# Second layer three pairs of blocks behind the first in place of two, and a shorter hold in the planner

## The chip, the cores and the metric

The kernel runs on one core of one Trainium2 chip. The metric is the device time of one execution in microseconds (us). One execution was also recorded by the hardware profiler; the instruction times below are from that record.

## The reference

A gated scan over the sequence feeds two feed-forward layers, on 12160 tokens (2 sequences of 6080) of 256 channels. All data is float32.

```python
f = lower_bound + (1 - lower_bound) * sigmoid(f_logit)
for t in range(S):                       # per sequence and channel
    h = f[:, t] * h + (1 - f[:, t]) * x[:, t];  y[:, t] = h
x = y.reshape(12160, 256)
x = square(relu(x @ w_in1)) @ w_out1     # layer 1: 256 -> 2048 -> 256
h = x @ w_in2                            # layer 2: 256 -> 2048 -> 256
out = where(h > 0, h, exp(min(h, 0)) - 1) @ w_out2
```

## The kernel before

**Blocks and slots.** The tokens are cut into 24 blocks, the first of 384 tokens and the others of 512 (`block_sizes`, L39). Each layer of a block is worked in 8 slots, one for each 256 of the 2048 hidden channels. Every value that goes into a matmul is kept as two fp32r parts, a high and a low one, and a product is three matmuls (high x high, high x low, low x high).

**What a slot does.** TensorE (PE) makes the first product into a PSUM tile `pc`, and later the second product from the tile `g` into `acc`. For layer 1 of the first four blocks (`PLAIN`, L22) the first product is the ordinary one: 12 matmuls of 512 columns (L640). All other slots use a scheme with 7 products of sums in place of 8: `first` is 9 matmuls, `later` is 12 (both L626), and between the two ScalarE copies part of `pc` away (`snap`, L654). ScalarE (ACT) and VectorE (DVE) then build the hidden values: DVE adds L657, L662, L669, L665 and ACT copies L672; layer 1 takes relu and square on ACT (L675, L678, or L647 and L678 in plain slots); layer 2 takes ACT L682 and L685 (exp) and DVE L688 (elu). At last ACT rounds to the high part of `g` (L693), DVE subtracts for the low part (L698), and PE makes the second product (L725), `LAG` = 3 slots later or earlier if the slot has aged. There is one L698 for each slot, so the L698 of DVE number the slots: 1 to 16 are the first pair of blocks in layer 1, 17 to 32 the second pair, and so on.

**Around the slots.** Each block needs a scan (two halves: loads `fs` and `xs`, ACT tanh L553, DVE transposes L558, gate L564, feed L572, scan L585, carry L591) into the tile `F`, and its operand parts `xA` or `xB` (sums L492, L496, L500 for the seven-product scheme, the high part by ACT L508 or by DVE L510, the low part by DVE L516). Layer 1's result is spilled to DRAM (`xd`) and loaded again as layer 2's `F`. The weights are prepared once, on the way: ACT L383 and L386, DVE L389, L392, then a high part (DVE L411 or ACT L409) and a low part (DVE L415). The sums of weights for the seven-product scheme (DVE L337 to L340, L351 or ACT L349, L354) are kept in DRAM (`wd`) and streamed from there; layer 1's sums are made from a copy in DRAM (`rd`, loaded at L457).

**What sets the order.** Blocks are worked in pairs, one layer of a pair being a run of 16 slots. The list of runs (L254 to L258) begins with `BEHIND` pairs of layer 1, then alternates a pair of layer 2 with the next pair of layer 1, and ends with `BEHIND` pairs of layer 2. PE's order follows from it alone (L267 to L292), and so do the due times of all steps: those of the weights are spread between the second pair's start and the first use (L836 to L844), and the scans of blocks from number `2 * BEHIND` on are held back to a slot of the run before (L870 to L875).

On the other engines the order is that of a planner (class `Order`, L47). It keeps for each engine the steps whose inputs it reckons ready. When the engine comes free, it looks at the steps that are ready then or within `HOLD` microseconds of the earliest, and takes the one with the earliest due time:

```python
t0 = max(free[e], min(r.values()))
n = min((n for n, t in r.items() if t <= t0 + self.HOLD), key=lambda n: steps[n][2])
```

Steps that may run on either of two engines (L508 or L510, L411 or L409, L349 or L351) go to the one that takes them first. The order so found is written out as each engine's instruction stream, and each engine works through its own in that order.

Of the kernel before, what the change touches and what calls it, by code (L numbers as in the profile page):

```python
# [19 lines left out]
LAST = ()  # L20
LEAD = 2
PLAIN = 4  # L22
BEHIND = 2
LAG = 3
AGE = 10.0
ROW = 1 / 2185
# [20 lines left out]
class Order:  # L47
# [6 lines left out]

    SAME, CROSS, LOAD = 0.13, 0.22, 2.4
    RATE, AHEAD = 240.0, 2.0
    HOLD = 0.2
    SLACK = 0.3

    def __init__(self):  # L60
# [33 lines left out]
    def run(self):  # L94
# [33 lines left out]
        while any(ready.values()):  # L128
            best = None
            for e, r in ready.items():  # L130
                if not r:
                    continue
                t0 = max(free[e], min(r.values()))
                n = min((n for n, t in r.items() if t <= t0 + self.HOLD), key=lambda n: steps[n][2])
                t0 = max(t0, r[n])
# [26 lines left out]
def kernel(  # L162
# [83 lines left out]
    def woven(m, bs, lead):  # L246
        a = [(m, bs[0], g) for g in range(KG)]
        b = [(m, x, g) for x in bs[1:] for g in range(KG)]
        got = a[:lead]
        for i in range(lead, KG + lead):  # L250
            got += a[i : i + 1] + b[i - lead : i - lead + 1]
        return got

    twos = [tuple(range(b, min(b + 2, NBK))) for b in range(0, NBK, 2)]  # L254
    runs = [(0, bs) for bs in twos[:BEHIND]]
    for i in range(BEHIND, len(twos)):
        runs += [(1, twos[i - BEHIND]), (0, twos[i])]
    runs += [(1, bs) for bs in twos[-BEHIND:]]  # L258
    slots = [s for m, bs in runs for s in woven(m, bs, LEAD)]
# [607 lines left out]
    for kind, s in pe_order:  # L867
        m, b, g = s
        if kind == "first":
            if m == 0 and g == 0:  # L870
                for h in range(2):

                    k = slots.index((0, b - b % 2, 0)) - SPREAD[b % 2 * 2 + h]
                    add_scan(n_scan, b, h, in_due[s] - 6.0, n_first[slots[k]] if b >= 2 * BEHIND else None)
                    n_scan += 1  # L875
# [45 lines left out]
```

## Time and profile before

| | |
|---|---|
| median of 3 runs | 2083.7 us (2083.47 to 2085.03) |
| the profiled execution's own time | 2083.75 us |
| its span, first to last instruction | 2082.0 us |
| PE busy | 2034.5 us, 98% of the span |
| DVE busy, ACT busy | 1732.3 us (83%), 1697.1 us (82%) |
| PE clock granted, mean | 0.996 of full |

PE is idle for 47.5 us of the span (2082.0 less 2034.5): at the start, in the stretch from 190 to 345 us, and in the last 20 us. In the 40 equal slices of the page, PE's first slice reads 3 and the rest 8 or 9.

### The profile page before, as it was taken

How to read it: one execution, taken by the hardware profiler on the slowest of the kernel's cores; microseconds unless marked ns; L12 is line 12 of the kernel's file. 1: busy time of each engine (PE TensorE's matmuls, PEld its weight loads, DVE VectorE, ACT ScalarE, POOL GpSimd, SP SyncE). 2: the span in 40 equal slices, each digit the busy share in tenths (PEclk: the TensorE clock that was granted, in tenths of full speed). 3: DMA queues.
4: the chain of work that ended last, by engine and by line, in shares of the span. 5: the costliest groups of instructions: out<-in, count | busy, mean ns of one | idle time of the engine just before them, and what ended most of it. 6: DMA issues, size and time to landing. Idle time of an engine off the chain costs nothing.

```text
span 2082.0 us, 36897 instructions
## 1 busy us (share of the span) xinstructions
PE 2034.5 (98%) x14640; PEld 1925.6 (92%) x14640; DVE 1732.3 (83%) x2830; ACT 1697.1 (82%) x2149; POOL 0.2 (0%) x4
## 2 busy tenths in 40 slices
PE   3999999999999999999999999999999999999998
PEld 3888889999999999999999999999999999999998
DVE  7977996996897798699699689779869968967876
ACT  5887778888888888889788888888888878888886
POOL 0000000000000000000000000000000000000000
PEclk8999999999999999999999999999999999999999
DMA  8787452442343344334244234334433424423321
GB/s 220 229 258 237 143 173 89 128 131 93 124 141 102 119 116 134 116 108 144 89 124 136 92 124 140 105 119 115 135 117 106 140 90 122 133 92 130 104 95 39
DMA packets 207540, 268.10 MB, mean 129 GB/s; under 512 B 110984, under 2 KB 135944, under 8 KB 207368
## 3 DMA queue, kind: packets, MB, share of 16 engines
q1 hardware_dynamic: 206784, 265.21, 40.7%
q8 instruction: 116, 1.90, 0.4%
q10 hardware_dynamic: 584, 0.53, 0.1%
q14 instruction: 56, 0.46, 0.1%
HBM read 221.91 MB, written 43.78 MB: 128 GB/s over the span
## 4 chain that ended last, share of the span: by engine, by line
PE 93%; DVE 4%; ACT 1%; DMA 1%; issue 0%; SPq 0%; DVEq 0%; ACTq 0%
PE acc L725 49%; PE pc L626 40%; PE pc L640 4%; DVE g L698 1%; DVE r L688 1%; DVE r L669 0%; DMA fs<-in_f_logit_dram 0%; DVE F L585 0%; ACT g L693 0%; DMA a<-rd 0%; DVE s L662 0%; ACT s L654 0%; SPq L328 0%; ACT e L682 0%; DVE r L665 0%
## 5 line engine op out<-in xcount | busy, mean ns | idle before, releaser
L725 PE MATMUL acc<-wo,g 128*128 128x256 f32 x4560 | 579.0, 282 | 4.4 <-DVE g L698 2.6
L725 PEld LDWEIGHTS acc<-wo,g 128*128 128x128 f32 x4560 | 560.1, 188 | 5.9 <-DVE g L698 3.9
L725 PE MATMUL acc<-g,wo 128*128 128x512 f32 (+1 forms) x2304 | 552.6, 389 | 0.0
L725 PEld LDWEIGHTS acc<-g,wo 128*128 128x128 f32 x2304 | 420.9, 188 | 78.5 <-DVE g L698 0.3
L626 PE MATMUL pc<-xB,ws 128*128 128x256 f32 x3696 | 486.9, 280 | 4.4 <-ACT s L654 3.6
L626 PE MATMUL pc<-xA,ws 128*128 128x256 f32 (+1 forms) x3696 | 485.8, 280 | 3.2 <-ACT s L654 2.0
L698 DVE TENSOR_TENSOR g<-r,g 128x1024 fp32r<-128x1024 f32 (+1 forms) x384 | 463.8, 1208 | 27.0 <-ACT g L693 24.7
L626 PEld LDWEIGHTS pc<-xB,ws 128*128 128x128 f32 x3696 | 463.6, 188 | 11.6 <-ACT s L654 4.2
L626 PEld LDWEIGHTS pc<-xA,ws 128*128 128x128 f32 x3696 | 463.0, 188 | 10.2 <-ACT s L654 2.4
L693 ACT ACTIVATE g<-r 128x1024 fp32r<-128x1024 f32 (+1 forms) x384 | 402.1, 1047 | 15.6 <-DVE r L688 8.6
L654 ACT ACTIVATE s<-pc 128x768 f32<-128x768 f32 (+1 forms) x352 | 283.5, 805 | 114.3 <-PE pc L626 112.8
L662 DVE TENSOR_TENSOR s<-pc,s 128x256 f32<-128x256 f32 (+1 forms) x352 | 147.8, 420 | 240.0 <-PE pc L626 238.7
L688 DVE SCALAR_TENSOR_TENSOR r<-e,r 128x1024 f32<-128x1024 f32 (+1 forms) x192 | 231.7, 1207 | 24.4 <-ACT e L685 23.7
L669 DVE TENSOR_TENSOR r<-pc,s 128x512 f32<-128x512 f32 (+1 forms) x352 | 241.8, 687 | 9.3
L682 ACT ACTIVATE e<-r 128x1024 f32<-128x1024 f32 (+1 forms) x192 | 202.0, 1052 | 15.0 <-DVE r L665 6.5
L685 ACT ACTIVATE e<-e 128x1024 f32<-128x1024 f32 (+1 forms) x192 | 202.1, 1052 | 6.0
L678 ACT ACTIVATE r<-r 128x1024 f32<-128x1024 f32 (+1 forms) x192 | 202.2, 1053 | 5.6
L675 ACT ACTIVATE r<-r 128x768 f32<-128x768 f32 x160 | 135.5, 847 | 77.7 <-DVE r L665 76.8
L672 ACT ACTIVATE r<-pc 128x256 f32<-128x256 f32 (+1 forms) x352 | 133.4, 379 | 79.5 <-DVE r L669 66.6
L657 DVE TENSOR_TENSOR s<-s 128x256 f32<-128x256 f32 (+1 forms) x352 | 147.1, 418 | 9.8 <-ACT s L654 0.8
L665 DVE TENSOR_TENSOR r<-s 128x256 f32<-128x256 f32 (+1 forms) x352 | 146.7, 417 | 0.0
L585 DVE TENSOR_TENSOR_SCAN F<-fT,carry,xT 128x256 f32<-128x256 f32 (+2 forms) x94 | 65.7, 728 | 0.3
(49 smaller groups left out, 832.1 us busy)
## 6 DMA issues: line engine op xcount, KB each, us to landing
ws<-wd SPq DMA_DIRECT2D x176, 896.0 KB, 5.0
out_dram<-o SPq DMA_DIRECT2D x47, 256.0 KB, 3.8
fs<-in_f_logit_dram SPq DMA_DIRECT2D x184, 64.0 KB, 3.9
xs<-in_x_dram SPq DMA_DIRECT2D x184, 64.0 KB, 2.1
xd<-o SPq DMA_DIRECT2D x46, 256.0 KB, 2.2
F<-xd SPq DMA_DIRECT2D x46, 256.0 KB, 3.3
st<-in_moe_w_out_dram SPq DMA_DIRECT2D x16, 512.0 KB, 4.6
wd<-wp SPq DMA_DIRECT2D x24, 256.0 KB, 4.0
```

The costliest lines, as they stand in the source:

```text
L626: nc.tensor.matmul(t["pc"][:, c], lhsT=ws[:, p, w], rhs=x_t[m, b][:, r, v], start=(which is FIRST_PRODUCTS and q == 0 and c in (1, 2)), st ...
L654: nc.scalar.activation(t["s"], t["pc"][:, 1:4], AF.Copy)
L657: nc.vector.tensor_tensor(t["s"][:, 1], t["s"][:, 1], t["s"][:, 2], op=ALU.add)
L662: nc.vector.tensor_tensor(t["s"][:, 0], t["pc"][:, 0], t["s"][:, 0], op=ALU.add)
L669: nc.vector.tensor_tensor(t["c"][:, 1:3], t["pc"][:, 2:4], u, op=ALU.add)
L678: nc.scalar.activation(t["r"], t["r"], AF.Square)
L682: nc.scalar.activation(t["e"], t["r"], AF.Relu, scale=-1.0)
L685: nc.scalar.activation(t["e"], t["e"], AF.Exp, scale=-1.0)
L688: nc.vector.scalar_tensor_tensor(t["r"], t["e"], 1.0, t["r"], op0=ALU.subtract, op1=ALU.max)
L693: nc.scalar.activation(t["g"][:, 0], t["r"], AF.Copy)
L698: nc.vector.tensor_tensor(t["g"][:, 1], t["r"], t["g"][:, 0].bitcast(F32), op=ALU.subtract)
L725: nc.tensor.matmul(a, lhsT=u, rhs=v, start=clear and k == 0, stop=two and k == 2, skip_group_check=True)
```

## The change

Two constants change. `BEHIND` goes from 2 to 3, `HOLD` from 0.2 to 0.1:

```diff
-BEHIND = 2
+BEHIND = 3
...
-    HOLD = 0.2
+    HOLD = 0.1
```

With `BEHIND` = 3 the runs are: layer 1 of pairs 0, 1, 2, then layer 2 of pair 0, layer 1 of pair 3, and so on, with three pairs of layer 2 at the end. The number of matmuls is the same. Both constants also move instructions on ACT, DVE and the DMA queue. DVE's high parts of x (L510) go from 27 to 34, ACT's (L508) from 65 to 58.

PE at the end of the second plain pair (`pc` first products, `acc` second products; `-` is the kernel before, `+` the changed one):

```order
 L725 MATMUL acc<-g,wo_70 128x512 x12
-L626 MATMUL pc<-xA,ws 128x192 x30
+L626 MATMUL pc<-xA,ws 128x256 x30
+L725 MATMUL acc<-g,wo_70 128x512 x12
+L626 MATMUL pc<-xA,ws 128x256 x21
+L725 MATMUL acc<-g,wo_70 128x512 x12
```

Where layer 2 of the first pair (192 columns wide) began, layer 1 of the third pair begins now.

DVE just before the first `xA` is ready, in the kernel before (`ws_235` and `ws_254` are the first layer's weights of slots 0 and 1, `F_221` the scan of block 0):

```order
L415 TENSOR_TENSOR ws_235<-a_198,ws_235 128x512
L392 SCALAR_TENSOR_TENSOR a_226<-st_193,a_226 128x512
L558 STREAM_TRANSPOSE fT_247<-fs_216 128x6x2x32
L564 TENSOR_SCALAR fT_247<-fT_247,ga_66,gb_67 128x192
L558 STREAM_TRANSPOSE xT_257<-xs_228 128x6x2x32
L564 TENSOR_SCALAR fT_247<-fT_247,ga_66,gb_67 128x192
L572 SCALAR_TENSOR_TENSOR xT_257<-fT_247,xT_257 128x2x192
L585 SCALAR_TENSOR_TENSOR F_221<-fT_247,carry_68,xT_257 128x192 x2
L591 COPY carry_68<-F_221 128x2
L389 SCALAR_TENSOR_TENSOR a_239<-a_239,st_204 128x512
L415 TENSOR_TENSOR ws_254<-a_226,ws_254 128x512
L516 TENSOR_TENSOR xA_269<-F_221,xA_269 128x4x192
```

The same place in the changed kernel (`ws_246` and `ws_269` are the weights of slots 1 and 2, `F_233` the scan):

```order
L411 CAST ws_246<-a_226 128x512
L415 TENSOR_TENSOR ws_246<-a_226,ws_246 128x512
L558 STREAM_TRANSPOSE fT_255<-fs_215 128x6x2x32
L558 STREAM_TRANSPOSE xT_257<-xs_228 128x6x2x32
L564 TENSOR_SCALAR fT_255<-fT_255,ga_66,gb_67 128x192
L389 SCALAR_TENSOR_TENSOR a_240<-a_240,st_204 128x512
L564 TENSOR_SCALAR fT_255<-fT_255,ga_66,gb_67 128x192
L392 SCALAR_TENSOR_TENSOR a_240<-st_204,a_240 128x512
L572 SCALAR_TENSOR_TENSOR xT_257<-fT_255,xT_257 128x2x192
L585 SCALAR_TENSOR_TENSOR F_233<-fT_255,carry_68,xT_257 128x192
L415 TENSOR_TENSOR ws_269<-a_240,ws_269 128x512
L585 SCALAR_TENSOR_TENSOR F_233<-fT_255,carry_68,xT_257 128x192
```

Ahead of the last scan instruction DVE now has eleven weight instructions (L389, L392, L411, L415) in place of six, and they stand between the scan's own steps; `L591` and `L516` come next.

DVE in a run of layer 2 in the middle of the kernel, where the next `xA` parts are made, before (`pc_12305` and `pc_12380` are first products of two slots that follow each other, `e` the exp):

```order
L698 TENSOR_TENSOR g_12356<-r_12250,g_12356 128x1024
L516 TENSOR_TENSOR xA_12320<-F_11674,xA_12320 128x1024
L662 TENSOR_TENSOR s_12347<-pc_12305,s_12347 128x256
L669 TENSOR_TENSOR r_12392<-pc_12305,s_12347 128x512
L688 SCALAR_TENSOR_TENSOR r_12349<-e_12376,r_12349 128x1024
```

And in the changed kernel:

```order
L662 TENSOR_TENSOR s_13164<-pc_13125,s_13164 128x256
L510 CAST xA_13215<-F_12507 128x1024
L688 SCALAR_TENSOR_TENSOR r_13166<-e_13194,r_13166 128x1024
L669 TENSOR_TENSOR r_13213<-pc_13125,s_13164 128x512
L657 TENSOR_TENSOR s_13243<-s_13243 128x256
L665 TENSOR_TENSOR r_13213<-s_13164 128x256
L516 TENSOR_TENSOR xA_13215<-F_12507,xA_13215 128x1024
```

The cast L510 was ACT's there, and now it and an elu stand between the two instructions that read one `pc`.

## Rows read from the trace of the kernel before

**Rows 1.** The page, part 1: busy us, share of the span, instructions.
```profile
PE 2034.5 (98%) x14640; PEld 1925.6 (92%) x14640; DVE 1732.3 (83%) x2830; ACT 1697.1 (82%) x2149; POOL 0.2 (0%) x4
```

**Rows 2.** Waits of PE, whole span: engine line <- releaser: us, times, longest.
```profile
PE pc L640 <- ACT xA L508: 20.5, 1, 20.5
PE pc L640 <- ACT xB L508: 10.1, 1, 10.1
```

**Rows 3.** Waits of PE from 190 to 345 us.
```profile
PE pc L626 <- ACT s L654: 5.6, 5, 1.7
PE pc L626 <- issue: 1.2, 1, 1.2
PE acc L725 <- DVE g L698: 1.0, 2, 0.8
PE pc L626 <- DVE r L669: 0.7, 1, 0.7
```

**Rows 4.** Windows of one run each: length, busy us by engine, clock, DMA share, GB/s.
```profile
209.00:293.67 84.67, 78.58 (x646) 76.78 (x644) 82.19 (x148) 64.36 (x90) 0.00 (x0) 1.00 0.50 158
...
378.34:463.01 84.67, 84.67 (x700) 84.14 (x699) 82.19 (x132) 71.33 (x90) 0.00 (x0) 1.00 0.44 131
463.01:547.68 84.67, 84.67 (x552) 77.31 (x551) 60.03 (x100) 70.06 (x91) 0.00 (x0) 1.00 0.32 106
```

**Rows 5.** DVE's groups by shape, 0 to 380 us: busy us, mean ns.
```profile
L392 DVE SCALAR_TENSOR_TENSOR a<-st,a 128x512 int32<-128x512 int32 x32 | 22.1, 690 | 0.8
L698 DVE TENSOR_TENSOR g<-r,g 128x768 fp32r<-128x768 f32 x16 | 15.2, 947 | 0.0
L411 DVE CAST wo<-a 128x512 fp32r<-128x512 f32 x15 | 6.4, 424 | 0.4
L337 DVE TENSOR_TENSOR a<-a 128x128 f32<-128x128 f32 x16 | 4.6, 287 | 8.0 <-DMA a<-rd 7.9
L510 DVE CAST xB<-F 128x1024 fp32r<-128x1024 f32 x2 | 1.4, 690 | 3.2 <-PE pc L640 3.2
```

**Rows 6.** Timeline of the start, ACT, DVE, PE: start us, us, instruction [idle before].
```profile
19.56 0.84 ACT L508 ACTIVATE xA<-F 128x768 fp32r<-128x768 f32 x1 [2.78 <-DVE F L585]
...
20.84 0.95 DVE L516 TENSOR_TENSOR xA<-F,xA 128x768 fp32r<-128x768 f32 x1
...
24.82 0.71 DVE L558 STREAM_TRANSPOSE xT<-xs 128x512 f32<-128x512 f32 x1
...
29.17 0.68 DVE L389 SCALAR_TENSOR_TENSOR a<-a,st 128x512 int32<-128x512 int32 x1
...
40.02 1.22 DVE L516 TENSOR_TENSOR xB<-F,xB 128x1024 fp32r<-128x1024 f32 x1
...
21.84 8.06 PE L640 MATMUL pc<-xA,ws 128*128 128x384 f32 x35 [0.70 <-DVE xA L516]
...
41.29 5.00 PE L640 MATMUL pc<-xB,ws 128*128 128x512 f32 x11 [0.51 <-DVE xB L516]
```

**Rows 7.** Timeline near the 14th slot, DVE's L698 and PE's second product.
```profile
101.71 1.22 DVE L698 TENSOR_TENSOR g<-r,g 128x1024 fp32r<-128x1024 f32 x1
...
106.83 2.90 PE L725 MATMUL acc<-g,wo 128*128 128x512 f32 x12
```

**Rows 8.** Waits of DVE, whole span.
```profile
DVE a L337 <- DMA a<-rd: 7.9, 3, 3.6
```

**Rows 9.** Timeline of PE at the first slot with seven products.
```profile
200.08 2.59 PE L626 MATMUL pc<-xA,ws 128*128 128x192 f32 x21 [0.74 <-ACT s L654]
```

**Rows 10.** Timeline late in a run of layer 2: PE's later product, DVE's L662.
```profile
797.62 2.66 PE L626 MATMUL pc<-xA,ws 128*128 128x256 f32 x21
...
801.05 0.42 DVE L662 TENSOR_TENSOR s<-pc,s 128x256 f32<-128x256 f32 x1
```

**Rows 11.** Waits of PE from 1990 us to the end.
```profile
PE acc L725 <- ACT g L693: 1.7, 1, 1.7
PE acc L725 <- DVE g L698: 1.6, 3, 0.8
```

## The prediction

> **What bounds the kernel now.** I read the busy shares first, then the windows of single runs, then the waits of PE, and last the timeline where PE waits. PE is busy for 2034.5 us of the 2082.0 us span [rows 1]. In the middle of the kernel one run of layer 2 and one of layer 1 take 84.67 us each, and PE is busy for all 84.67 us of both [rows 4]. There a change that keeps the number of matmuls can win nothing; it can only break something. What can be won is PE's 47.5 us of idle time. It lies in three places: 20.5 us before the first product and 10.1 us before the first product on `xB` [rows 2]; 5.6 + 1.2 + 1.0 + 0.7 = 8.5 us between 190 and 345 us [rows 3]; and 1.7 + 1.6 = 3.3 us at the end [rows 11]. The rest, some 5 us, is short waits at the start and the time after the last matmul.
>
> The 8.5 us have a cause that the windows show. A run of layer 2 alone keeps DVE busy for 82.19 of its 84.67 us; the first such run, from 209 us on, shows the same 82.19 us of DVE, but only 78.58 us of PE [rows 4]. In the order, between the 32nd and the 48th L698, DVE has weight work on top: 13 instructions of 512 columns (L389, L392, L415, L354), 3 casts and 16 sums of 128 columns. At 0.690, 0.424 and 0.287 us [rows 5] that is 9.0 + 1.3 + 4.6 = 14.9 us in a run that has some 2.5 us free. The narrower first block gives part of it back; the rest PE waits for, and clears it in the next run.
>
> **The third pair in between: -8.5 us.** The order of the changed kernel puts a run of layer 1 there. Such a run needs 60.03 us of DVE [rows 4]; the third sixteen slots now hold 14 of the long weight instructions, 3 casts and 8 sums, 9.7 + 1.3 + 2.3 = 13.3 us, so 73 of 84.67 us. The run of layer 2 after it holds no weight instruction at all and is like those of the middle, where PE doesn't wait. I take away all 8.5 us. The bounds are 0 and 8.5.
>
> **What is late in its place: +2.3 us.** Two places, from the order.
> - The first slot with seven products has its `first` and `later` products next to each other on PE, so PE must wait for the copy between them: 0.74 us today [rows 9]. The same gap stays. ACT now has an L508 for `xB` between the last plain slot's relu and that copy, an instruction of 0.84 us on the smaller block [rows 6]; I add 0.6 us of it and take 1.3 us.
> - The first layer's sums are due sooner and the scans of the third pair come a run earlier. Before its 14th L698 DVE has more to do than today: one scan of half a block, 29.17 - 24.82 = 4.35 us [rows 6]; four sums, 1.15 us; two casts L351, 0.85 us; three long instructions, 2.07 us; less two casts L411, 0.85 us [rows 5]. That is 7.6 us. Today this L698 ends at 102.93 and PE needs its tile at 106.83, 3.9 us later [rows 7]; with PE 3.1 us later (below) the cover is 7.0 us. So 0.6 us are left over. The sums read DRAM, and such reads made DVE wait up to 3.6 us [rows 8]; behind the waiting sum stands this very L698, and PE behind that. I take 0.8 us, bounds 0 and 4.2.
> - 0.2 us for others. Together 2.3 us; the bounds are 0.7 us, today's one wait, and 8.5 us, as much as goes.
>
> **The start: +3.1 us.** This is the shorter hold. DVE no longer keeps itself free for the next step of the scan, but fills each gap with a weight instruction of half a microsecond or more. Ahead of the end of block 0's scan stand eleven weight instructions in place of six: four more of 0.690 and one of 0.424 us [rows 5], 3.2 us. Two that stood between scan and L516 are among them, so L516 now waits only for ACT's L508, 0.84 us [rows 6]. I went through both queues instruction by instruction, with each duration as the timeline has it and with the gaps it shows between instructions that depend on each other and those that don't (the mixed order saves some of these gaps). L516 for `xA`, at 20.84 us today, comes 2.0 us later, and PE's 21.84 us with it [rows 6]. From there to L516 for `xB`, at 40.02 us today, two more L698 of 0.947 us stand in the way, one L389 more and one L411 less, 2.2 us [rows 5], of which the saved gaps give back more than half: 0.9 us more. PE starts on `xB` at about 44.2 us in place of 41.29 us [rows 6], 2.9 us later; with 0.2 us for ACT, which is late too, I take 3.1 us. By durations alone it would be 2.8 + 2.2 = 5.0 us; the least is the 2.0 us of the first part. A gain is excluded, since nothing is taken out of the way. From there to the 13th slot I found no product that comes late: DVE has the L698 of three slots behind it when PE resumes, and one today.
>
> After its wait PE runs at the lower of its two clocks: 5.00 us for 11 matmuls, 0.455 us each [rows 6], against 2.90 / 12 = 0.242 us later [rows 7]. That costs 2.3 us, and it will again, since the wait stays about as long: 0, bounds -1.2 and +1.2 us.
>
> **The middle: 0.** The hold changes the order of ACT and DVE in every run. DVE takes seven more casts L510 (27 to 34). In runs of layer 2 an L510 or a piece of a scan, and an elu, stand more often between L662 and L669, which together free a `pc`. Today, late in such a run, `later` ends at about 799.06 us and L662 starts at 801.05 us, 2.0 us behind [rows 10], and PE doesn't notice. PE needs that tile again one slot later, 84.67 / 16 = 5.3 us; L662 and L669 take some 1.1 us, so DVE may be about 4.2 us late. Adding up DVE's work slot by slot through one run of the new order, I find it at most 1.9 us behind, plus 1.8 us for a cast and an elu in front of L669: 3.7 us. It fits, barely.
>
> A rule of the Trainium skill speaks against the change here: its page Perfetto Trace Analysis, section Optimizing Scalar/DVE Operations, says that where DVE is saturated, moving work to Scalar may pay, and this change moves seven casts the other way. By that rule each would cost PE its 0.690 us, 4.8 us in all, and the sum would be 2085.1 us. By the rows PE is full beside a DVE at 82.19 of 84.67 us, so they cost nothing, and I go by the rows.
>
> **The end: -0.3 us.** The last run is as before; going through its last three slots I find the last product 0.3 us sooner. Bounds -1.6 and +1.0.
>
> **The sum.** The profiled execution took 2083.75 us, 0.05 us above the median of the runs, so nothing is corrected. 2083.75 - 8.5 + 2.3 + 3.1 - 0.3 = 2080.35, so 2080.3 us.
>
> **Rivals.**
> - *A cheap start.* The start costs 2.0 us and only the 0.7 us wait is new: 2083.75 - 8.5 + 0.7 + 2.0 - 0.3 = 2077.7 us. For it: DVE's two loads fall to 73 us of 84.67. Against it: the 14th slot has no cover to spare. 24%.
> - *The jam moves and doesn't go.* The second plain run takes over four half scans, 4 x 4.35 = 17.4 us, beside sums that wait for DRAM; DVE carries its lateness into the third run, whose first slots are its fullest, and PE waits 6 us there instead: 2084.0 us. Against it: that third run has 11 us to spare. 18%.
> - *The middle breaks: slower.* In the nine runs of layer 2 that also carry scans, L669 comes more than 4.2 us after `later` ends, once a run, and PE waits for its `pc`, say 1.2 us, the length of a single wait in [rows 3]: 9 x 1.2 = 10.8, so 2091 us. For it: 3.7 of 4.2 us; it decides from 0.5 us more. Against it: nothing in today's middle comes near. 12%.
>
> The forecast has 46%, with its own range from 2078.5 to 2082.3 us. A measurement of this kernel can tell about 0.2%, 4.2 us, from no change: below 2079.5 us is faster, above 2087.9 us slower. Faster: nearly all of the cheap start and a third of the forecast, 0.38. Slower: the broken middle, 0.11. Within: 0.51. The range from 2076.8 to 2085.2 us leaves out the broken middle and a few per cent of the bounds.
>
> **What would show it.** Right: PE's first wait near 23 us and its start on `xB` near 44 us; almost no PE wait from 210 us on; one wait for L654 near 203 us; runs of 84.67 us with PE full. Wrong: PE waits for L669 or L654 in runs of layer 2 after 400 us (broken middle), several waits between 200 and 300 us (the jam moved), or a start on `xB` near 41 or beyond 46 us.

## The result and the profile after

The changed kernel takes 2095.33 us in the median of four runs (2093.97 to 2096.27), the kernel before 2084.27 us in the four beside them: a ratio of 1.0053 with an interval of 1.0035 to 1.0070. It is slower, and 10 us above the upper end of the range. The profiled execution took 2094.52 us, its span is 2092.7 us, 10.7 us longer than before. The matmuls did not grow (PE is busy for 2036.0 us, 2034.5 before), so the loss is idle time. The waits of PE over the whole span answer to [rows 2, 3, 11]:

```profile
PE pc L640 <- ACT xA L508: 23.2, 1, 23.2
PE pc L640 <- ACT xB L508: 11.2, 1, 11.2
PE pc L626 <- ACT s L654: 9.0, 5, 4.4
PE acc L725 <- DVE g L698: 6.7, 11, 1.1
PE pc L640 <- ACT r L647: 1.6, 1, 1.6
```

Two lines carry the result. L654, the copy between `first` and `later`, is waited for 9.0 us in place of 5.6, once for 4.4 us. L698, the product that the output matmuls need, is waited for eleven times in place of five.

Where the 10.7 us are is read from the first L725 of each run of slots, in the two timelines:

| stretch | before, us | after, us | difference |
|---|---|---|---|
| up to the first L725 | 46.13 | 48.40 | +2.27 |
| plain runs and the first run with seven products in layer 1 (83.43 us elsewhere) | 164.25 + 83.43 | 254.75 | +7.07 |
| first run of layer 2 | 92.04 | 90.08 | -1.96 |
| run of layer 1 behind it | 83.82 | 83.43 | -0.39 |
| seven repeated runs of layer 2 | 85.92 each | 86.70 each | +5.45 |
| the rest, to the end | | | -1.71 |

A repeated run of layer 2 and one of layer 1 together take 169.35 us before, twice the 84.67 us of [rows 4]; cut at the first L725 they are 85.92 and 83.43 us long.

**The third run, +7.07 us.** Three timelines of the kernel after, PE, ACT and DVE, show its worst place (start us, us, instruction, idle before):

```profile
202.57 1.22 PE L626 MATMUL pc<-xA,ws 128*128 128x256 f32 x9
208.19 4.08 PE L626 MATMUL pc<-xA,ws 128*128 128x256 f32 x21 [4.41 <-ACT s L654]
...
201.76 0.63 ACT L409 ACTIVATE wo<-a 128x512 fp32r<-128x512 f32 x1 [2.78 <-DVE a L392]
202.29 1.07 ACT L790 ACTIVATE o<-acc 128x512 f32<-128x512 f32 x2
203.25 1.03 ACT L647 ACTIVATE r<-pc 128x1024 f32<-128x1024 f32 x1
204.15 0.85 ACT L508 ACTIVATE xB<-F 128x768 fp32r<-128x768 f32 x1
204.88 1.06 ACT L678 ACTIVATE r<-r 128x1024 f32<-128x1024 f32 x1
205.83 0.67 ACT L383 ACTIVATE a<-st 128x512 f32<-128x512 f32 x1
206.38 1.06 ACT L693 ACTIVATE g<-r 128x1024 fp32r<-128x1024 f32 x1
207.33 0.81 ACT L654 ACTIVATE s<-pc 128x768 f32<-128x768 f32 x1
...
201.03 0.69 DVE L392 SCALAR_TENSOR_TENSOR a<-st,a 128x512 int32<-128x512 int32 x1
```

PE's nine `first` products are done at 203.8 us. L654 could copy them then, but stands in ACT's queue behind all the rows shown above it. The queue had stood still for 2.78 us behind L409, the rounding of a weight to its high part, for which DVE had not yet delivered the weight (L392). A similar stop of ACT, 2.81 us long until 184.74 us, lies before PE's wait of 1.59 us for L647 at 188.39. Before, this cast stood on DVE at both places (L411): of the sixteen for `wo`, ACT had one, now it has six. And the long wait costs more than itself. The windows of the kernel after around it (length, busy us of PE, PEld, DVE, ACT, POOL, then the clock):

```profile
190.00:202.00 12.00, 12.00 (x53) 9.52 (x52) 11.69 (x22) 8.84 (x12) 0.00 (x0) 1.00 0.64 237
202.00:208.00 6.00, 1.79 (x13) 1.46 (x11) 4.68 (x6) 6.00 (x9) 0.00 (x0) 0.98 0.61 185
208.00:212.00 4.00, 3.81 (x21) 3.81 (x22) 3.14 (x6) 1.34 (x3) 0.00 (x0) 0.60 1.03 343
```

Having stood for 4.41 us, PE comes back at a mean clock of 0.60, most of that stretch at the lower of its two levels (1.2 GHz): its 21 products take 4.08 us, where 21 of the same kind take 2.63 to 2.77 us.

**The first run of layer 2, -1.96 us.** It was to get back nearly all of [rows 3]. DVE has no weight work there any more, and PE waits almost as before. The window of this run, after [rows 4]:

```profile
303.15:393.23 90.08, 83.99 (x695) 82.33 (x694) 81.25 (x141) 68.94 (x95) 0.00 (x0) 1.00 0.40 123
```

PE is idle for 6.1 us of 90.08, DVE for 8.8. PE waits for L654 four times in this run, before and after. One of these waits, PE's timeline before and then after:

```profile
234.68 1.26 PE L626 MATMUL pc<-xB,ws 128*128 128x256 f32 x9
237.01 1.68 PE L626 MATMUL pc<-xB,ws 128*128 128x256 f32 x12 [1.08 <-ACT s L654]
```

```profile
327.14 1.24 PE L626 MATMUL pc<-xB,ws 128*128 128x256 f32 x9
329.91 1.70 PE L626 MATMUL pc<-xB,ws 128*128 128x256 f32 x12 [1.53 <-ACT s L654]
```

The nine `first` and the twelve `later` products of one slot stand next to each other in PE's own order, with no output product between, so PE must wait until ACT has read the nine. By the code this comes from L283 (an experiment below changes it): the narrow first block gets its output products out earlier (its age is scaled by 384/512), and the next slots have none left to put in between.

**The repeated runs, +5.45 us.** PE and DVE of the kernel after, at the end of one of them:

```profile
552.78 2.90 PE L725 MATMUL acc<-wo,g 128*128 128x256 f32 x22 [0.55 <-DVE g L698]
...
548.84 0.42 DVE L657 TENSOR_TENSOR s<-s 128x256 f32<-128x256 f32 x1
549.17 0.42 DVE L665 TENSOR_TENSOR r<-s 128x256 f32<-128x256 f32 x1
549.51 0.16 DVE L591 COPY carry<-F 128x2 f32<-128x2 f32 x1
549.57 0.42 DVE L496 TENSOR_TENSOR F<-F 128x256 f32<-128x256 f32 x1
550.03 0.43 DVE L500 TENSOR_TENSOR F<-F 128x256 f32<-128x256 f32 x1
550.37 1.22 DVE L516 TENSOR_TENSOR xB<-F,xB 128x1024 fp32r<-128x1024 f32 x1
551.51 1.22 DVE L698 TENSOR_TENSOR g<-r,g 128x1024 fp32r<-128x1024 f32 x1
```

DVE works without a gap, and ahead of the product that is due stand 2.2 us of preparation for a later block. PE waits 0.54 us, once per run, in seven of them; the 24 products, broken in two, take 3.30 us of PE in place of 3.04, and the run is 0.78 us longer. At the same place of the kernel before, 75.18 us after the first L725 of the run, that L698 stands ahead of the scan and was done 2 us before PE needed it (DVE, then PE):

```profile
458.03 1.23 DVE L698 TENSOR_TENSOR g<-r,g 128x1024 fp32r<-128x1024 f32 x1
459.17 1.39 DVE L585 TENSOR_TENSOR_SCAN F<-fT,carry,xT 128x256 f32<-128x256 f32 x2
...
461.42 3.04 PE L725 MATMUL acc<-wo,g 128*128 128x256 f32 x24
```

### The profile page after: what moved, and what is told of

Same layout as the page of the kernel before. It is cut to its first block, busy times and chain, and to the rows that moved or that the text cites. A ratio compares the mean times of both kernels' runs of the same rounds, so it can differ in the third digit from the quotient of the medians.

```text
span 2092.7 us, 36829 instructions
## 1 busy us (share of the span) xinstructions
PE 2036.0 (97%) x14640; PEld 1926.3 (92%) x14640; DVE 1715.1 (82%) x2833; ACT 1688.2 (81%) x2146; POOL 0.2 (0%) x4
## 4 chain that ended last, share of the span: by engine, by line
PE 67%; DVE 23%; ACT 4%; DMA 3%; issue 2%; SPq 1%; DVEq 0%; ACTq 0%
PE acc L725 35%; PE pc L626 31%; DVE g L698 5%; DVE r L688 3%; DVE r L669 2%; DVE F L585 1%; DVE s L657 1%; DVE s L662 1%; DVE r L665 1%; DVE xA L516 1%; DMA st<-in_moe_w_out_dram 1%; ACT s L654 1%; ACT e L685 1%; ACT e L682 1%; DVE fT L564 1%
## 5 line engine op out<-in xcount | busy, mean ns | idle before, releaser
L725 PE MATMUL acc<-wo,g 128*128 128x256 f32 x4560 | 581.0, 283 | 7.1 <-DVE g L698 6.7
L725 PEld LDWEIGHTS acc<-wo,g 128*128 128x128 f32 x4560 | 560.7, 189 | 10.1 <-DVE g L698 9.2
L725 PE MATMUL acc<-g,wo 128*128 128x512 f32 (+1 forms) x2304 | 552.5, 389 | 0.0
L725 PEld LDWEIGHTS acc<-g,wo 128*128 128x128 f32 x2304 | 420.9, 188 | 78.1 <-DVE g L698 0.4
L698 DVE TENSOR_TENSOR g<-r,g 128x1024 fp32r<-128x1024 f32 (+1 forms) x384 | 463.6, 1207 | 17.1 <-ACT g L693 15.6
L662 DVE TENSOR_TENSOR s<-pc,s 128x256 f32<-128x256 f32 (+1 forms) x352 | 147.5, 419 | 277.8 <-PE pc L626 277.5
L654 ACT ACTIVATE s<-pc 128x768 f32<-128x768 f32 (+1 forms) x352 | 283.0, 804 | 54.1 <-PE pc L626 52.7
L669 DVE TENSOR_TENSOR r<-pc,s 128x512 f32<-128x512 f32 (+1 forms) x352 | 240.2, 682 | 9.0 <-ACT r L672 4.0
L657 DVE TENSOR_TENSOR s<-s 128x256 f32<-128x256 f32 (+1 forms) x352 | 147.0, 418 | 10.7 <-ACT s L654 1.8
```

The lines of the kernel that those rows point to most:

```text
L654: nc.scalar.activation(t["s"], t["pc"][:, 1:4], AF.Copy)
L657: nc.vector.tensor_tensor(t["s"][:, 1], t["s"][:, 1], t["s"][:, 2], op=ALU.add)
L662: nc.vector.tensor_tensor(t["s"][:, 0], t["pc"][:, 0], t["s"][:, 0], op=ALU.add)
L669: nc.vector.tensor_tensor(t["c"][:, 1:3], t["pc"][:, 2:4], u, op=ALU.add)
L698: nc.vector.tensor_tensor(t["g"][:, 1], t["r"], t["g"][:, 0].bitcast(F32), op=ALU.subtract)
L725: nc.tensor.matmul(a, lhsT=u, rhs=v, start=clear and k == 0, stop=two and k == 2, skip_group_check=True)
```

## Experiments

Ten kernels, each timed in three rounds beside the kernel before. The stops given are PE's idle times as its timeline lists them, those with a named releaser and those called issue.

**One constant at a time.**

```diff
-    HOLD = 0.1        # the kernel after, BEHIND = 3
+    HOLD = 0.2
```

> The kernel after with HOLD back at 0.2 (BEHIND 3 alone). Theory A, HOLD does the harm: the start goes back to 46.1 us (-2.3), the 0.5 us stop of TensorE for DVE's product g in each repeated second-layer run goes (-5.5), and since only two of the sixteen wo casts stand on ACT (six with HOLD 0.1) the stops of 1.6 and 4.4 us at 188 and 208 and the slower clock behind them go (-7.0): 2095.3 - 14.8 = 2080.5 us. Theory B, the third pair itself does it (its block pair has no second-layer work beside it that gives time): the start alone comes back, 2093 us. In between, about 2087.5, if only the repeated runs come back.

2080.97 us, ratio 0.998 (0.9971 to 0.9989).

```diff
-    HOLD = 0.2        # the kernel before, BEHIND = 2
+    HOLD = 0.1
```

> The kernel before with HOLD 0.1 (HOLD alone). Theory A: +2.3 at the start and +0.78 in each of nine repeated second-layer runs, 2084.3 + 9.3 = 2093.6 us, more if a stop by a wo cast on ACT comes on top. Theory B, the third pair does it: start alone, 2086.6 us.

2091.27 us, ratio 1.0032 (1.0020 to 1.0044).

| | first L725 | stops 60 to 430 us | 430 to 2000 | behind 2000 |
|---|---|---|---|---|
| before | 46.13 | 8.6 | 0 | 3.3 |
| BEHIND 3 alone | 46.31 | 5.7 | 0 | 3.3 |
| HOLD 0.1 alone | 48.40 | 7.4 | 4.4 | 1.8 |
| after | 48.40 | 11.9 | 3.8 | 1.8 |

The third pair alone gains 3.4 us. HOLD costs 2.3 us at the start and some 0.8 us in each of eight or seven repeated runs, with either BEHIND. Against 2084.41 us, -3.4 and +6.9 make +3.5; both together gave +11. So some 7.5 us are neither's: the stop at 188 us is in neither of the two profiles, and where the one of 4.41 us stands they have 0.9 us (BEHIND alone) and 0.7 us (HOLD alone). HOLD alone has six casts for `wo` on ACT too, as the changed kernel has, so their number alone doesn't make the stops.

**Who makes the stops at 188 and 208 us?**

```diff
-            ["DVE", dve(CE, True), high_part, [a], [w], ("ACT", act(CE))],
+            ["DVE", dve(CE, True), high_part, [a], [w], *([("ACT", act(CE))] if kind == 0 else [])],
```

> The kernel after with the high part of the output weights (wo) always on DVE, where the planner could give it to ACT and did in six of sixteen. Theory A: the stops of TensorE of 1.59 us (for ACT's r at 188) and 4.41 us (for ACT's s at 208) go, with the 1.6 us of slower clock behind, since nothing on ACT waits for DVE's weight steps there: 2095.3 - 7.6 = 2087.7 us. Rival: DVE is the full engine there, takes six casts of 0.42 us more (2.5 us), is as late as before, and the stop only changes its name: 2094 to 2097 us.

2091.11 us: 4.2 us less than after, not 7.6. The waits of ACT from 170 to 215 us, after and then with this edit:

```profile
ACT wo L409 <- DVE a L392: 5.6, 2, 2.8
ACT wp L349 <- DVE a L392: 3.1, 3, 1.7
```

```profile
ACT wp L349 <- DVE a L392: 8.6, 3, 3.9
```

With this kind of cast forbidden, the casts of the kept parts on ACT (L349, 16 in place of 15) wait instead, and ACT stands as long, but ahead of other instructions: PE stands for 2.8 us in place of 6.0, and at full clock (1.00 from 203 to 214 us). So I took all weight casts from ACT:

```diff
-            ["DVE", dve(CE, True), high_part, [key], [w], ("ACT", act(CE))],
+            ["DVE", dve(CE, True), high_part, [key], [w]],
-            ["DVE", dve(CE, True), high_part, [a], [w], ("ACT", act(CE))],
+            ["DVE", dve(CE, True), high_part, [a], [w]],
```

> The kernel after with every high part of a weight (wo, ws and the kept parts wp: 48 casts) on DVE, 22 of which stood on ACT. With wo alone moved, ACT still waited 8.6 us for DVE's L392 before the wp casts between 170 and 215 us, and TensorE stood 2.8 us of 7.6. Theory A in full (ACT held back by casts of weights that DVE delivers late): no ACT instruction waits for a weight step there, the stops for ACT's r and s between 180 and 212 sum to at most 1.2 us, 2095.3 - 6.4 = 2088.9 us or less. Rival: DVE itself, with 0.42 us more for each of 22 casts, is late; 2 to 3 us of stops for DVE's g or for s behind it stay, 2091 us or more.

2091.60 us. PE's waits from 110 to 220 us with this edit:

```profile
PE pc L626 <- ACT s L654: 2.2, 2, 1.4
PE acc L725 <- DVE g L698: 0.3, 1, 0.3
```

2.5 us are left of 6.0 and the slow clock; the first L725 comes at 50.08 us, 1.7 us later, with the casts at the start on DVE too. So some 5 of the 7.6 us are the casts on ACT with the clock behind them. The edit also shifts the rest of the order, so this is a sum over the stretch and not the price of one cast. With BEHIND alone the stop is 0.9 us; the 1.6 us between that and 2.5 come with HOLD 0.1 and are not the casts. ACT's timeline of this run says what the two waits for L654 hang on:

```profile
200.39 1.03 ACT L647 ACTIVATE r<-pc 128x1024 f32<-128x1024 f32 x1 [2.20 <-PE pc L640]
201.31 0.84 ACT L508 ACTIVATE xB<-F 128x768 fp32r<-128x768 f32 x1
...
204.65 0.79 ACT L654 ACTIVATE s<-pc 128x768 f32<-128x768 f32 x1
...
210.64 0.38 ACT L672 ACTIVATE r<-pc 128x256 f32<-128x256 f32 x1 [4.63 <-DVE s L662]
```

Before the first, of 1.36 us, ACT waits for PE itself, and four instructions, with the L508 for `xB` the first, stand between L647 and the copy. Before the second, of 0.80 us, ACT waits for DVE's L662, which came behind two weight instructions (L389, L392): there the rival holds.

**TensorE's own order, in the kernel before.**

```diff
-        while pending and (not s or i - pending[0][0] >= LAG or now - pending[0][2] >= AGE * sizes[pending[0][1][1]] / TB):
+        while pending and (not s or i - pending[0][0] >= LAG or now - pending[0][2] >= AGE):
```

> The kernel before with the age at which an output product is due no longer scaled by the block's width, which changes TensorE's order only around the 384-wide block: between the first and the later products of every second-layer slot there is then output work (before, four slots of the first run have none). Theory C: the stops of the first second-layer run come from TensorE's own order, not from DVE's weight load, and 6 to 8 us go: 2084.3 - 7 = 2077.3 us. Rival, the reading of the prediction (DVE's load of the last w_out and w_rec tiles sets it): the stops stay, 2084 us; or the order of the narrow block in the plain runs costs as much as is gained, also 2084.

2084.43 us, no change (0.9989 to 1.0007), and both theories were right in part. The stops for L654 went from 5.6 to 0.7 us. In their place stands one of 6.9 us, which the profile calls issue. PE and DVE of this kernel there:

```profile
295.17 2.26 PE L626 MATMUL pc<-xA,ws 128*128 128x256 f32 x9 [6.90 <-issue]
...
292.28 1.39 DVE L585 TENSOR_TENSOR_SCAN F<-fT,carry,xT 128x256 f32<-128x256 f32 x2
293.71 0.69 DVE L492 TENSOR_TENSOR F<-F 128x512 f32<-128x512 f32 x1
294.32 0.16 DVE L591 COPY carry<-F 128x2 f32<-128x2 f32 x1
294.39 0.68 DVE L669 TENSOR_TENSOR r<-pc,s 128x512 f32<-128x512 f32 x1
```

L669, the last reader of a `pc`, ends at 295.07 and PE starts at 295.17; that it is the releaser is read from these times. DVE, full since 281 us, is within 0.6 us of where it was before, when PE waited 1.2 us there [rows 3]. So with two pairs PE's order is not the only limit of this run: mend it, and PE waits about as long for DVE, full with weights and scans. How much of that is the weights and how much the place of L669, which has a half scan between itself and L662, this run doesn't separate. If it is the weights, only PE's order is left with three pairs, and the same edit should pay:

> BEHIND 3, HOLD 0.2 and the age unscaled (the run with BEHIND alone, and TensorE's order mended at the narrow block). Theory C with DVE free: in the kernel before the mended order took the stops for s from 5.6 to 0.7 us, but TensorE then waited 6.9 us for DVE's r (L669) at 295, which comes no earlier as DVE is full there. With the third pair DVE has no weight work in the first second-layer run, so nothing takes the stops' place: of 4.7 us of stops for s some 3.8 go, 2081.0 - 3.8 = 2077.2 us. Rival: DVE's gate steps alone set that run, TensorE waits again for r, 2081 us.

BEHIND 3, HOLD 0.2, age unscaled: 2076.75 us, ratio 0.9964 (0.9949 to 0.9978). PE's timeline at the place shown above:

```profile
327.76 1.26 PE L626 MATMUL pc<-xB,ws 128*128 128x256 f32 x9
328.85 2.32 PE L725 MATMUL acc<-wo,g 128*128 128x256 f32 x18
331.01 1.59 PE L626 MATMUL pc<-xB,ws 128*128 128x256 f32 x12
```

From 210 to 2000 us PE has no wait. (The profiled run, the longest of five, took 2079.0 us and has a stop of 2.7 us at 202 us.)

**The repeated runs: the casts on DVE, or the order?**

```diff
-            ["ACT", act(4 * n), high(0, 4, 0), [T, *ready], [X[0]], ("DVE", dve(4 * n, True))],
+            ["ACT", act(4 * n), high(0, 4, 0), [T, *ready], [X[0]]],
```

> The kernel after with the larger of the two casts of the inputs' high parts (2048 and 1536 columns in two pieces, L508 on ACT or L510 on DVE) given to ACT alone: 3 of these casts on DVE in place of 34. Theory D, the extra casts on DVE make its product g late in the repeated second-layer runs: the 0.54 us stop goes in each of seven, -5.5 us, 2089.8 us. Theory A, it is the finer weaving of scan and part steps between the gate's steps that HOLD 0.1 makes, with no cast standing among them at the stop: the stop stays at 0.5 us in each, 2094 to 2096 us. ACT, which gets 31 casts of about 0.95 us, could become late and make it slower, 2098 us or more.

2094.09 us: the stop stays, 0.36 to 0.41 us in each of eight runs. So these casts make at most 0.13 to 0.18 us of it. The load isn't the cause either: in a repeated run of layer 2 DVE is busy for 83.4 to 83.6 us before, without a stop, and for 83.6 to 83.7 us after. What differs is the order, as the rows above show. The edit also cut the stops from 188 to 207 us to 3.6 us in place of 6.0, with six casts for `wo` still on ACT: DVE has 31 casts fewer over the kernel, and ACT waits there at one L409 for L392 (2.8 us) in place of two.

**HOLD the other way.**

```diff
-    HOLD = 0.2        # BEHIND 3, age unscaled
+    HOLD = 0.4
```

> As the run with HOLD 0.2 and the age unscaled, with HOLD 0.4: scans wait longer for steps that are due sooner or the other way round. Theory A (a larger HOLD keeps a chain of scan steps together on DVE, a smaller weaves weight steps into it): the first input xA is ready sooner, the start falls below 46.1 us by 1 to 2.5 us, 2075.5 us. Rival: with 46 of the input casts on DVE in place of 28 the repeated runs get a stop on DVE, +0.5 to 0.8 in each of sixteen, 2085 us or more.

2084.67 us. Both came true: the first L725 at 43.04 us, 3.1 us sooner, and a stop in each of eight repeated runs, this time for L669, with 3.6 us more around 370 us. Of those, 3.1 us stand where the 6.9 us above stood, with L669 behind a half scan again and no weight instruction in the run, so there the order alone is enough to stop PE. PE's waits from 400 to 1990 us:

```profile
PE pc L626 <- DVE r L669: 4.2, 8, 0.5
```

So 0.1 and 0.4 both break the middle and 0.2 doesn't; at the start the larger is the better. Hence one value for each:

```diff
-                n = min((n for n, t in r.items() if t <= t0 + self.HOLD), ...
+                n = min((n for n, t in r.items() if t <= t0 + (0.4 if t0 < 60.0 else self.HOLD)), ...
```

> BEHIND 3, age unscaled, HOLD 0.4 up to 60 us of the planner's time and 0.2 after. If HOLD acts in the two places independently, the first output product comes at 43.0 us as with HOLD 0.4 (46.2 with 0.2) and the repeated runs have no stop, as with 0.2: 2076.8 - 3.1 = 2073.7 us. Rival: the rest of the order shifts with the start and a stop of 0.5 us in each second-layer run returns, 2079 us.

2075.37 us, ratio 0.9955 (0.9940 to 0.9970). The start gives the 3.1 us and the middle has no stop, but the medians are only 1.4 us apart, with intervals that overlap (the two profiled runs are 3.1 us apart). The stops for L654 at 197 and 205 us are 3.7 us here, the second of them, 2.3 us, behind one L349 at which ACT waits 5.8 us for DVE's L392.

> As the run before it, with every high part of a weight on DVE. Theory A: the stop of 0.9 to 2.7 us for ACT's s at 202 goes, 2072.5 us. Rival: DVE's 22 added casts of 0.42 us lie in the stretch in which it is full, and cost 2 to 4 us: 2076 us.

2074.44 us, ratio 0.9952 (0.9937 to 0.9967): the fastest, though not told apart from the one before it. The stops from 60 to 430 us fall from 3.7 to 1.8 us, the 2.3 us among them to 0.4 (a stop of 0.9 us at 198 us stays), and the first L725 comes 0.8 us later.

## Why the prediction was wrong

**The third pair in between, -8.5 us: failed, measured -2.4 us in the two runs.** That DVE is full there was read correctly, and the run with the age unscaled shows it. The wrong step was from there to "the rest PE waits for": five of the waits were for L654 behind nine products with no other work in between, which the names in [rows 3] say, and they have PE's order as a second cause: with the third pair the run still had four of them, and they went when L283 was changed. I counted DVE's work per run and did not look at what stood between `first` and `later`, though I did so for the one slot in [rows 9]. The run after it is "like those of the middle" in its DVE work only; the narrow block is still in it.

**What is late in its place, +2.3 us: failed, +7.1 us.** Of its parts, the 0.8 us at the 14th slot didn't come. The first slot with seven products was to cost 1.3 us for one L508 more ahead of the copy; it cost 4.4 us, and another 1.6 us came at 188 us. With every weight cast off ACT the first of these is 1.36 us, so the L508 was priced rightly and what was missing is the casts. I had counted that casts left DVE (L411) and credited DVE with them, and did not follow them to ACT, where each waits for DVE with the queue behind it. The slower clock after the stop was not in the sum at all.

**The middle, 0: failed, +5.45 us.** I followed L669 and the time until its `pc` is needed, and found 3.7 of 4.2 us. That product is in time; the one late is L698, whose deadline I didn't work out. The rival of the broken middle had the place, but nine runs for seven, the wrong instruction, and 1.2 us for 0.54 to 0.78. The rule of the Trainium skill that I weighed (Perfetto Trace Analysis, Optimizing Scalar/DVE Operations) would have put the loss on the seven casts; giving them and more to ACT left 0.4 us of each stop, so the size was near (4.8 us for 5.45) by luck, and the reason was another.

**The start, +3.1 us: right in mechanism, measured +2.27.** The first wait was to be near 23 us and the start on `xB` near 44.2. PE's timeline after, against [rows 6]:

```profile
43.07 0.79 PE L640 MATMUL pc<-xB,ws 128*128 128x512 f32 x1 [11.21 <-ACT xB L508]
44.43 4.14 PE L640 MATMUL pc<-xB,ws 128*128 128x512 f32 x11 [0.56 <-DVE xB L516]
```

44.43 us. The 0.9 us that are missing are in the eleven products behind it: 4.14 us in place of 5.00, as the clock came back earlier: 0.65 over these products in place of 0.52. I had put 0 +/- 1.2 us on that.

**The end, -0.3 us: mis-sized, -1.7 us**, 0.1 us beyond the lower bound of -1.6.

Two rivals came true together: the jam moved to the third run (7.1 us for the 6 it named, but through ACT's queue and not by DVE's lateness alone), and the middle broke. I had given them chances as alternatives, 18% and 12%, and no case for both, though one constant causes the second and helps the first.

## What to carry to other kernels

When a planner may give a step to either of two engines, follow the moved step into the queue that receives it: an in-order queue stops at an instruction whose input is late, and all that stands behind it is late with it, whatever the busy shares say. Before counting a wait as gained, ask for each instruction that waits what stands between it and what it waits for on its own engine; a wait can have two causes, and then they have to be removed together: here PE's order alone gained nothing, the third pair alone 3.4 us, and both 7.9. Change one constant of a planner at a time: here one gained 3 us, the other cost 7, and together they cost 7.5 us more.

## What the runs showed of the hardware

After single stops of PE of up to 1.6 us the granted clock was 1.00 in the windows read here. After longer ones it differed from place to place:

| stop | granted clock behind it | what the products behind it took |
|---|---|---|
| 6.90 us (295 us, kernel before with the age unscaled) | 0.50 over 2.3 us | 9 of 256 columns in 2.26 us in place of 1.3 |
| 4.41 us (208 us, above) | 0.60 over 4 us | 21 in 4.08 us in place of 2.77 |
| 2.66 us (202 us, HOLD 0.2, age unscaled) | 0.69 over 4 us | 21 in 3.64 us, the next 12 in 3.64 in place of 2.9 |
| 2.26 us (205 us, HOLD by time) | 0.64 over 4 us | 21 in 3.98 us, the next 12 in 3.25 |
| 3.11 us (370 us, HOLD 0.4) | 1.00 over 3.35 us | 24 of 256 columns in 3.04 us, none slower |
| 0.51, 0.87, 1.07 us (229 to 233 us, HOLD alone) | 0.62 over 7.6 us | 40 of 256 columns in 7.60 us, where 24 take 3.04 |

So the length of a stop didn't tell by itself whether the clock fell; behind the stops of 4.41, 2.66 and 2.26 us the products took 1.3 to 1.6 us longer. Narrow products save little: twelve `later` products of 192 columns take 1.48 us on PE and twelve of 256 columns 1.58 to 1.59 us.
